# Clustered attention with a squared-ReLU MLP: another order of the opening (scales, centroids, first loads)

## The chip, the cores and the metric

The kernel runs on one core of a Trainium2 chip. The metric is the device time of one execution in microseconds. Its engines are PE (TensorE, matmuls), DVE (VectorE), ACT (ScalarE), POOL (GpSimd) and SP, which here issues all transfers.

## The reference

```python
def _attn_ref(q, k, v, centroids):            # q, k, v: 4 x 8 x 768 x 64; centroids: 8 x 16 x 64
    q_n = q / (norm(q) + 1e-06); k_n = k / (norm(k) + 1e-06); c_n = centroids / (norm(centroids) + 1e-06)
    q_assign = argmax(einsum('bhsd,hcd->bhsc', q_n, c_n), -1)
    k_assign = argmax(einsum('bhsd,hcd->bhsc', k_n, c_n), -1)
    mask = q_assign[:, :, :, None] == k_assign[:, :, None, :]
    scores = where(mask, (1 / sqrt(D)) * q @ k.T, -1e9)
    scores = scores - max(scores, -1)
    attn = exp(scores); attn = attn / (sum(attn, -1) + 1e-09)
    return attn @ v
def _moe_ref(x, w_in, w_out, s, b):           # x: 3072 x 512, w_in: 512 x 2048, w_out: 2048 x 512
    r = maximum(x @ w_in, 0.0)
    return (s * (r * r) + b) @ w_out
```

Each query attends only to the keys whose nearest centroid is the same as its own. The heads' outputs are laid side by side and go through the MLP. All inputs are float32.

## The kernel before

**The arithmetic.** Operands are scaled by a power of two and split into a high and a low float16 part, so that PE works on float16. For this, each operand needs its largest absolute value: DVE reduces along the free axis (`absmax`), PE spreads the column over all partitions (`allmax`, a matmul with the identity), DVE reduces again, and three short DVE rows (`scale2`, lines 68 to 70) make the scale of it. `split` (lines 178 to 187) then makes the high part on ACT and the low part on DVE.

**Masks.** The clusters enter the scores as extra columns: after a DMA transpose of the split keys (KA) or queries (QA), PE multiplies them by the transposed centroids cT, DVE makes a one-hot of the best cluster (`onehot`, lines 281 to 292), and this is written into a second operand, which is transposed in its turn (KB, QB). A unit's score matmuls (line 464) take QA with KA and QB with KB.

**Units and the loop.** A unit is one head, one batch and one tile of 128 queries: 192 units in all. The loop at line 709 goes over units i: score matmuls of unit i, maximum over 768 keys on DVE (line 473), exponential on ACT (line 483), transposes of the result, and the product with the values five units later. The scores have two buffers of PSUM. 21 units later the MLP of a pair of tiles begins, in steps of 128 columns of the hidden layer (lines 583, 590 to 593, 598, 610).

**Weights.** The MLP needs the largest value of all weights before its first step. The 32 weight tiles of 512 KB (w_in and w_out by turns) come through three staging buffers; for each one, ACT makes a float32 out of the loaded words (`rebase`, line 203), DVE puts the remaining bits in (`narrow`, lines 207 and 208), and ACT and PE or ACT alone bound its size (`bound`). A staging buffer is free for the next load once its tile is narrowed. Line 242, `finish_w_in`, is the first row behind the last w_in tile. The first three loads are issued in the opening, the others in the loop, two steps of the generator `weights` in each round.

**The opening.** Before the loop, lines 683 to 706 drive generators by hand: `prep_k` for the four pairs of heads of the keys (`first_k`), `prep_q` for the two halves of the first queries (`first_q`), `prep_v`, and `weights`. Each `next` takes a generator to its next `yield`: the load; absmax and allmax; scale and high part; low part and the transpose KA or QA; centroid matmuls and one-hot; the mask and the transpose KB or QB. `second` are the generators of the keys of the third and fourth pairs and of the second half of the queries.

**What sets the order.** A scheduler puts the instructions of each engine in order by priorities in the order of the program text and its own estimate of when operands are there. `behind(x, ...)` tells it to place what is inside only after the given instructions. So the order of each engine is fixed when the program is built, and an engine waits at each row until that row's operands are there, whatever stands behind it. SP issues transfers in its own fixed order too.

Of the kernel before, what the change touches and what calls it, by code (L numbers as in the profile page):

```python
# [14 lines left out]
ALU = mybir.AluOpType  # L15
# [11 lines left out]
def tile_cluster_attention_mlp(ctx, tc, q, k, v, cent, w_in, w_out, s_in, b_in, out):  # L27
    nc = tc.nc
    B, H, S, _ = q.shape
# [10 lines left out]
    V = nc.vector  # L40
# [25 lines left out]
    def scale2(dst, src):  # L66
        bits = dst.bitcast(I32)
        V.tensor_scalar(bits, src.bitcast(I32), EXPMASK, None, op0=ALU.bitwise_and)  # L68
        V.tensor_scalar(bits, bits, -1, 253 << 23, op0=ALU.mult, op1=ALU.add)
        V.tensor_scalar(dst, dst, 2.0 ** 60, None, op0=ALU.min)  # L70


    last_transpose = [None]
    last_turn = [None]
    last_split = [None, None]
    last_score = [None]
    last_max = [None]
# [45 lines left out]
    def scalar_in(src, name):  # L123
        every = const([P, 1], F32, name)
        nc.sync.dma_start(every, src.partition_broadcast(P))
        return every

    def behind(*last):
        stack = ExitStack()
        for ins in last:  # L130
            if ins is not None:
                stack.enter_context(tc.issue_after(ins.ins))
        return stack
# [7 lines left out]
    V.tensor_tensor(csq, cn, cn, op=ALU.mult)  # L141
    V.tensor_reduce(cs[:, 0:1], csq, axis=AX.X, op=ALU.add)
    A.activation(cs[:, 1:2], cs[:, 0:1], AF.Sqrt)
    for _ in range(3):
        V.tensor_scalar(cs[:, 1:2], cs[:, 1:2], 1e-30, None, op0=ALU.max)
        V.reciprocal(cs[:, 2:3], cs[:, 1:2])
        V.scalar_tensor_tensor(cs[:, 1:2], cs[:, 0:1], cs[:, 2:3], cs[:, 1:2], op0=ALU.mult, op1=ALU.add)
        V.tensor_scalar(cs[:, 1:2], cs[:, 1:2], 0.5, None, op0=ALU.mult)
# [157 lines left out]
    def prep_k(b, hp):  # L306
        kb = kb_kept
        if b == 0 and hp > 0:
            kb = sb.tile([P, 2 * T, P], F16, tag="big", name=f"kb_{hp}", bufs=BIGN).rearrange("p (h t) (e d) -> p h t e d", h=2, e=2)
        n = f"{b}_{hp}"  # L310
        kn = sb.tile([P, 2, T, D], F32, tag="kv", name=f"kn_{n}", bufs=5)
        load(kn, k[b, 2 * hp : 2 * hp + 2].rearrange("h (p t) d -> p h t d", t=T))
        yield
        if b:
            yield from until(START[b][2] if hp == 0 else step[0] + 1)
        if hp == 0:
            KSM[b] = sb.tile([P, 4, NP], F32, tag="ksm", name=f"ksm_{n}", bufs=2)
        sm = [KSM[b][:, e, hp : hp + 1] for e in range(4)]
        km = columns(1, f"k{n}")
        absmax(km, kn.rearrange("p h t d -> p (h t d)"))  # L320
        if b:
            yield
        allmax(sm[1], km, f"k{n}", "m" if b or not hp else "h")
        yield
        scale2(sm[2], sm[1])
        inverse2(V, sm[3], sm[2], 22)
        if b == 0 and hp > 0:
            ka = sb.tile([P, 2 * T, P], F16, tag="big", name=f"ka_{hp}", bufs=BIGN).rearrange("p (h t) (e d) -> p h t e d", h=2, e=2)
        else:
            ka = sb.tile([P, 2, T, 2, D], F16, tag="big", name=f"ka_{n}", bufs=BIGN)  # L330
        yield from split(ka[:, :, :, 0, :], ka[:, :, :, 1, :], kn, sm[2], False)
        G.tensor_copy(kb[:, :, :, 0, :], ka[:, :, :, 0, :])
        KA = sb.tile([P, 2 * T, P], F16, tag="KA", name=f"KA_{n}", bufs=5)
        KB = sb.tile([P, 2 * T, P], F16, tag="KB", name=f"KB_{n}", bufs=5)
        KS[(b, hp)] = (KA, KB)
        last_turn[0] = nc.sync.dma_start_transpose(KA, ka.rearrange("p h t e d -> p (h t e d)"))
        yield
        yield
        pa = (ps_m if b or not hp else ps_h).tile([P, 512], F32, tag="m" if b or not hp else "h", name=f"pk_{n}")
        for h in range(2):  # L340
            hc = slice((2 * hp + h) * C, (2 * hp + h + 1) * C)
            for t in range(T):
                i = h * T + t
                o = pa[:, i * C : (i + 1) * C]
                nc.tensor.matmul(o, KA[:, i, :], cT[:, 0, hc], start=True, stop=False)
                nc.tensor.matmul(o, KA[:, i, :], cT[:, 1, hc], start=False, stop=True)
        mk = kb.rearrange("p h t e (r c) -> p (h t) e r c", c=C)[:, :, 1, :, :]
        yield from onehot(pa, 2 * T, f"k{n}", mk, BIG, -BIG, G if b or hp > 1 else V)
        last_turn[0] = nc.sync.dma_start_transpose(KB, kb.rearrange("p h t e d -> p (h t e d)"))

    def prep_q(b, c, hq):
# [8 lines left out]
        sm = sb.tile([P, 4, 2], F32, tag="qsm", name=f"qsm_{n}", bufs=3)  # L360
# [11 lines left out]
        qa = sb.tile([P, 2 * T * P], F16, tag="big", name=f"qa_{n}", bufs=BIGN)[:, : nh * CT * 2 * D].rearrange("p (h t e d) -> p h t e d", h=nh, t=CT, e=2)  # L372
# [10 lines left out]
        QA = sb.tile([P, nh * CT, P], F16, tag="QA", name=f"QA_{n}", bufs=2)  # L383
        QB = sb.tile([P, nh * CT, P], F16, tag="QB", name=f"QB_{n}", bufs=2)
        QS[(b, c, hq)] = (QA, QB, sm)
        nc.sync.dma_start_transpose(QA, qa.rearrange("p h t e d -> p (h t e d)"))
        yield
        yield
        pa = (ps_m if b or c else ps_h).tile([P, 512], F32, tag="m" if b or c else "h", name=f"pq_{n}")
# [260 lines left out]
    wgen = weights()  # L650
# [4 lines left out]
    def run(gen):  # L655
        for _ in gen:
            pass

    def some(gen, n):
        for _ in range(n):  # L660
            next(gen, None)


    def prepare(k):
        if k == 0:
            with behind(last_transpose[0]):
                for gen in second:
                    next(gen)
        with behind(last_score[0], last_exp[0], last_max[0]):
            if k == 1:  # L670
                run(first_k[2])
                some(first_v, 1)
            if k == 2:
                run(first_k[3])
                some(first_v, 1)
            if k == 3:
                run(first_q[1])
                some(first_v, 2)
            if k == 4:
                some(first_v, 1)  # L680
                active.append(first_v)

    first_v = prep_v(0)
    first_k = [prep_k(0, hp) for hp in range(NP)]
    first_q = [prep_q(0, 0, hq) for hq in range(2)]
    second = [first_k[2], first_k[3], first_q[1]]
    for gen in (first_k[0], first_q[0], first_k[1], *second):
        next(gen)
    some(first_k[0], 2)
    some(first_k[1], 2)  # L690
    some(first_q[0], 2)
    some(first_k[0], 1)
    some(first_q[0], 1)
    some(first_k[1], 1)
    with behind(*last_split):
        for _ in range(2):
            for gen in second:
                next(gen)
    with behind(last_turn[0], *last_split):
        some(first_v, 1)  # L700
        sv = scalar_in(s_in, "sv")
        bv = scalar_in(b_in, "bv")
        some(wgen, 3)
    run(first_k[0])
    run(first_q[0])
    run(first_k[1])
    last_transpose[0] = last_turn[0]
    i = 0
    while i < NU + 8 or i - LAG < NS + 4:
# [61 lines left out]
```

## Time and profile before

| | |
|---|---|
| median of 3 runs | 953.16 us (952.39 to 954.72) |
| the profiled execution | 953.86 us, of which the profile's span is 952.2 us |
| instructions in the span | 22467 |
| first score matmul | 27.17 us |
| first maximum of scores | 34.85 us |
| first row behind the last w_in tile (line 242) | 131.37 us |
| first MLP matmul (line 583) | 133.81 us |

Times inside the span are read from its start. A busy engine may still work on what nobody waits for, so the stages have to be read one by one: the windows give each engine's busy time in a stretch, and the rows in order of time give in brackets for how long the engine had been idle and what it had waited for.

### The profile page before, as it was taken

What the parts mean: (1) busy time and instruction counts of PE and PEld (TensorE: products, weight loads), DVE (VectorE), ACT (ScalarE), POOL (GpSimd) and SP (SyncE); (2) the same over time, 40 slices, a digit from 0 to 9 for tenths busy, and PEclk for the clock granted to TensorE, in tenths of its full rate; (3) what the DMA queues carried; (4) which work ended last, traced back from release to release, by engine and by line L of the source; (5) the groups of instructions that cost most, each with busy time, mean ns of one, the idle gap of its engine ahead of it and who ended that gap; (6) DMA issues with size and microseconds to landing.
All of it is one profiled execution on the core that took longest, in us unless ns stands there. A gap on an engine that the chain in (4) does not pass through costs nothing. (4 is left out here: it accounts for less than half of the span.)

```text
span 952.2 us, 22467 instructions
## 1 busy us (share of the span) xinstructions
PE 828.6 (87%) x8625; PEld 579.4 (61%) x8625; DVE 626.1 (66%) x1400; ACT 711.0 (75%) x1390; POOL 573.0 (60%) x596
## 2 busy tenths in 40 slices
PE   0668446988999989999899999999999999999997
PEld 0457324555666667766566666766666766767764
DVE  7797988999677657767865757668666466463100
ACT  4477656887688778987787877978787888789443
POOL 3012545677578566866767758667776765676321
PEclk9965556999999999999999999999999999999999
DMA  6888974876887796968689969758877757777100
GB/s 182 227 215 234 235 179 92 197 151 114 174 167 154 170 201 122 186 147 181 139 165 177 184 142 181 149 130 189 156 153 170 145 116 152 138 165 133 33 23 22
DMA packets 450300, 147.36 MB, mean 155 GB/s; under 512 B 417937, under 2 KB 446609, under 8 KB 450193
## 3 DMA queue, kind: packets, MB, share of 16 engines
q1 hardware_dynamic: 450192, 145.93, 72.2%
q8 instruction: 67, 1.10, 0.5%
q14 instruction: 41, 0.33, 0.1%
HBM read 35.69 MB, written 6.29 MB: 44 GB/s over the span
## 5 line engine op out<-in xcount | busy, mean ns | idle before, releaser
L506 POOL TENSOR_TENSOR ph<-p,ph 128x768 f16<-128x768 f32 x184 | 312.2, 1697 | 123.7 <-ACT ph L119 76.2
L583 PE MATMUL h<-x,wis 128*128 128x256 f16 x2304 | 287.6, 274 | 9.6 <-ACT r L590 8.0
L610 PE MATMUL acc<-wos,g 128*128 128x512 f16 x1152 | 292.6, 379 | 3.2 <-POOL g L598 2.8
L583 PEld LDWEIGHTS <-wis 128*128 128x128 f16 x2304 | 222.2, 98 | 59.5 <-issue 11.3
L598 POOL TENSOR_TENSOR g<-r,g 128x256 f16<-128x256 f32 x192 | 136.6, 713 | 101.7 <-ACT r L593 97.1
L473 DVE TENSOR_REDUCE ssm<-sc 128x1 f32<-128x768 f32 x192 | 181.5, 951 | 24.4 <-PE sc L464 23.6
L483 ACT ACTIVATE p<-sc,ssm,qsm 128x768 f32<-128x768 f32 x192 | 187.7, 978 | 3.4 <-DMA PT<-ph 1.0
L610 PEld LDWEIGHTS <-g 128*128 128x128 f16 x1152 | 103.6, 97 | 87.8 <-POOL g L598 5.7
L480 ACT ACTIVATE ssm<-ssm,lift,qsm 128x1 f32<-128x1 f32 x192 | 73.1, 381 | 92.5 <-DVE ssm L473 91.7
L119 ACT ACTIVATE ph<-p 128x768 f16<-128x768 f32 x164 | 136.1, 830 | 5.8 <-DMA PT<-ph 4.3
L590 ACT ACTIVATE r<-h,cf 128x256 f32<-128x256 f32 x192 | 89.1, 464 | 56.9 <-PE h L583 49.6
L525 PE MATMUL px<-vh,PT 128*128 128x65 f16 x1104 | 120.4, 197 | 12.9 <-DVE xs L537 6.8
L464 PE MATMUL sc<-KA,QA 128*128 128x384 f16 x384 | 99.9, 343 | 26.4 <-ACT p L483 23.4
L526 PE MATMUL px<-vl,PT 128*128 128x64 f16 x1104 | 120.3, 194 | 0.0
L527 PE MATMUL px<-vh,PT 128*128 128x65 f16 x1104 | 120.0, 195 | 0.0
L525 PEld LDWEIGHTS <-PT 128*128 128x128 f16 x1104 | 103.6, 98 | 23.1 <-issue 14.4
L526 PEld LDWEIGHTS <-PT 128*128 128x128 f16 x1104 | 103.3, 100 | 13.2 <-issue 5.1
L464 PE MATMUL sc<-KB,QB 128*128 128x384 f16 x384 | 100.1, 345 | 7.0 <-DMA QB<-qb 7.0
L527 PEld LDWEIGHTS <-PT 128*128 128x128 f16 x1104 | 103.5, 98 | 2.7
L592 ACT ACTIVATE g<-r 128x256 f16<-128x256 f32 x192 | 79.3, 413 | 4.0
L593 ACT ACTIVATE r<-r 128x256 f32<-128x256 f32 x192 | 78.8, 411 | 3.3
L464 PEld LDWEIGHTS <-QA 128*128 128x128 f16 x384 | 35.9, 101 | 54.9 <-issue 29.2
(156 smaller groups left out, 1032.3 us busy)
## 6 DMA issues: line engine op xcount, KB each, us to landing
wst<-in_moe_w_in_dram SPq DMA_DIRECT2D x16, 512.0 KB, 4.5
wst<-in_moe_w_out_dram SPq DMA_DIRECT2D x16, 512.0 KB, 4.5
kn<-in_k_dram SPq DMA_DIRECT2D x16, 384.0 KB, 4.1
qn<-in_q_dram SPq DMA_DIRECT2D x24, 256.0 KB, 3.5
vn<-in_v_dram SPq DMA_DIRECT2D x16, 384.0 KB, 4.1
out_dram<-o SPq DMA_DIRECT2D x12, 512.0 KB, 3.8
PT<-ph SPq DMA_TRANSPOSE x184, 3.5
x<-xn SPq DMA_TRANSPOSE x48, 2.5
```

The source lines that it names most:

```text
L119: A.activation(dst, src, AF.Copy)
L464: last_score[0] = nc.tensor.matmul(sc[:, e, :HALF], X[:, col, :], y[:, h * S + e * HALF : h * S + (e + 1) * HALF], start=st, stop=not st)
L473: last_max[0] = V.tensor_reduce(SM[i // 4][:, 0, j : j + 1], U[i]["sc"], axis=AX.XY, op=ALU.max, negate=True)
L483: last_exp[0] = A.activation(p.rearrange("p (a b) -> p a b", a=2), u["sc"], AF.Exp, bias=bi, scale=u["scale"], **total)
L506: G.tensor_tensor(u["ph"][:, 1, :], u["p"], u["ph"][:, 0, :], op=ALU.subtract)
L525: nc.tensor.matmul(o1, PT[:, kt, :], vh[:, h, kt, : D + 1], start=(kt == 0), stop=False)
L526: nc.tensor.matmul(o, PT[:, kt, :], vl[:, h, kt, :], start=False, stop=False)
L527: nc.tensor.matmul(o1, PT[:, T + kt, :], vh[:, h, kt, : D + 1], start=False, stop=(kt == T - 1))
L583: nc.tensor.matmul(ph[:, :CW], WSP[ft][0][:, wl, kt, :], XS[(b, c, kt)][:, :, xl, :], start=(i == 0), stop=(i == len(terms) - 1))
L590: A.activation(r, ph[:, :CW], AF.Relu, scale=MS[(b, c)][0])
L598: G.tensor_tensor(g[:, 1, :], r, g[:, 0, :], op=ALU.subtract)
L610: nc.tensor.matmul(acc[:, t, :], g[:, gl, rows], WSP[ft][1][:, wl, :], start=(ft == 0 and gl + wl == 0), stop=(ft == NF - 1 and gl == 1))
```

## The change

Five things in the opening are put in another place, and one step of a root is dropped.

```diff
@@ scale2
-        V.tensor_scalar(dst, dst, 2.0 ** 60, None, op0=ALU.min)
+        return V.tensor_scalar(dst, dst, 2.0 ** 60, None, op0=ALU.min)
@@ centroids
-    for _ in range(3):
+    for _ in range(2):
         V.tensor_scalar(cs[:, 1:2], cs[:, 1:2], 1e-30, None, op0=ALU.max)
         V.reciprocal(cs[:, 2:3], cs[:, 1:2])
...
@@ prep_k
-        scale2(sm[2], sm[1])
+        last_scale[0] = scale2(sm[2], sm[1])
@@ prep_q
-        nc.sync.dma_start_transpose(QA, qa.rearrange("p h t e d -> p (h t e d)"))
+        last_q[0] = nc.sync.dma_start_transpose(QA, qa.rearrange("p h t e d -> p (h t e d)"))
@@ prepare
             if k == 1:
                 run(first_k[2])
+                some(first_q[1], 1)
                 some(first_v, 1)
             if k == 2:
                 run(first_k[3])
+                some(first_q[1], 1)
                 some(first_v, 1)
@@ the opening
-    second = [first_k[2], first_k[3], first_q[1]]
+    second = [first_k[2], first_k[3]]
     for gen in (first_k[0], first_q[0], first_k[1], *second):
         next(gen)
     some(first_k[0], 2)
-    some(first_k[1], 2)
+    with behind(last_scale[0]):
+        some(first_k[1], 2)
     some(first_q[0], 2)
     some(first_k[0], 1)
     some(first_q[0], 1)
     some(first_k[1], 1)
-    with behind(*last_split):
+    with behind(last_q[0], *last_split):
+        some(first_v, 1)
+        sv = scalar_in(s_in, "sv")
+        bv = scalar_in(b_in, "bv")
+        next(first_q[1])
+        some(wgen, 2)
         for _ in range(2):
             for gen in second:
                 next(gen)
-    with behind(last_turn[0], *last_split):
-        some(first_v, 1)
-        sv = scalar_in(s_in, "sv")
-        bv = scalar_in(b_in, "bv")
-        some(wgen, 3)
     run(first_k[0])
     run(first_q[0])
     run(first_k[1])
+    some(wgen, 1)
     last_transpose[0] = last_turn[0]
```

The maximum of the second keys is placed behind the first keys' scale. The root of the centroids' squared norms takes two Newton steps instead of three. The loads of the first values, of s and b, of the first two weight tiles and of the second half of the queries are placed behind the first transpose QA of the queries; the third weight load comes after the first one-hots. The second half of the queries is no longer prepared in the opening but in the first rounds of the loop.

In the rows below a line of the changed kernel stands two higher than the same line before, and the last number of a name is a running number. SP, the opening's transfers. kn, qn, vn are loads of keys, queries and values, wst of weights; KA, KB, QA, QB and cT are transposes. Before:

```order
L336 DMA_TRANSPOSE KA_0_1_205<-ka_1_171 128x12x128
L82 DMA vn_0_0_250<-in_v_dram 128x2x384
L125 DMA sv_252<-in_moe_s_dram 128x1
L125 DMA bv_254<-in_moe_b_dram 128x1
L82 DMA wst_0_257<-in_moe_w_in_dram 128x4x256
L160 DMA_TRANSPOSE cT_126<-cnat_120 128x3x128
L82 DMA wst_1_260<-in_moe_w_out_dram 128x1024
L82 DMA wst_2_266<-in_moe_w_in_dram 128x4x256
L386 DMA_TRANSPOSE QA_0_0_0_200<-qa_0_0_0_186 128x8x128
L349 DMA_TRANSPOSE KB_0_0_195<-kb_131 128x12x128
L399 DMA_TRANSPOSE QB_0_0_0_201<-qb_0_0_0_187 128x8x128
```

The same stretch after:

```order
L162 DMA_TRANSPOSE cT_122<-cnat_116 128x3x128
L338 DMA_TRANSPOSE KA_0_1_199<-ka_1_165 128x12x128
L351 DMA_TRANSPOSE KB_0_0_189<-kb_127 128x12x128
L388 DMA_TRANSPOSE QA_0_0_0_194<-qa_0_0_0_180 128x8x128
L84 DMA vn_0_0_203<-in_v_dram 128x2x384
L127 DMA sv_205<-in_moe_s_dram 128x1
L127 DMA bv_207<-in_moe_b_dram 128x1
L84 DMA qn_0_0_1_209<-in_q_dram 128x4x128
L84 DMA wst_0_212<-in_moe_w_in_dram 128x4x256
L84 DMA wst_1_215<-in_moe_w_out_dram 128x1024
L84 DMA wst_2_340<-in_moe_w_in_dram 128x4x256
L401 DMA_TRANSPOSE QB_0_0_0_195<-qb_0_0_0_181 128x8x128
```

QA now stands ahead of the loads of values and weights, and the first KB stands ahead of QA; the load of the second queries (qn_0_0_1), once among the first loads of the program, has come behind QA.

DVE, the rows that end in the query's mask qb, which QB transposes. pq are the query's products with the centroids, pk_0_1 those of the second keys. Before:

```order
L208 SCALAR_TENSOR_TENSOR wi1_265<-wst_2_266,wi1_265 128x512
L286 TENSOR_REDUCE om_q0_0_0_320<-pq_0_0_0_303 128x8
L287 TENSOR_TENSOR oe_q0_0_0_321<-pq_0_0_0_303,om_q0_0_0_320 128x128
L289 TENSOR_TENSOR oe_q0_0_0_321<-oe_q0_0_0_321,rev_73 128x128
L290 TENSOR_REDUCE om_q0_0_0_320<-oe_q0_0_0_321 128x8
L291 TENSOR_TENSOR oo_q0_0_0_322<-oe_q0_0_0_321,om_q0_0_0_320 128x128
L286 TENSOR_REDUCE om_k0_1_355<-pk_0_1_330 128x12
L292 TENSOR_SCALAR qb_0_0_0_187<-oo_q0_0_0_322 128x8x64
```

After:

```order
L288 TENSOR_REDUCE om_q0_0_0_291<-pq_0_0_0_274 128x8
L189 SCALAR_TENSOR_TENSOR ka_3_237<-kn_0_3_142,ksm_0_0_144,ka_3_237 128x12x64
L289 TENSOR_TENSOR oe_q0_0_0_292<-pq_0_0_0_274,om_q0_0_0_291 128x128
L291 TENSOR_TENSOR oe_q0_0_0_292<-oe_q0_0_0_292,rev_73 128x128
L292 TENSOR_REDUCE om_q0_0_0_291<-oe_q0_0_0_292 128x8
L209 TENSOR_SCALAR wi0_211<-wi0_211 128x512
L293 TENSOR_TENSOR oo_q0_0_0_293<-oe_q0_0_0_292,om_q0_0_0_291 128x128
L288 TENSOR_REDUCE om_k0_1_326<-pk_0_1_301 128x12
L210 SCALAR_TENSOR_TENSOR wi0_211<-wst_0_212,wi0_211 128x512
L294 TENSOR_SCALAR qb_0_0_0_181<-oo_q0_0_0_293 128x8x64
```

Before, all three first weight tiles are narrowed ahead of the query's one-hot; now the narrowing of the first (L209, L210) stands inside it, and that of the second and third tile behind the mask.

ACT, the rows around the exponential of the third unit, p_2. Before:

```order
L119 ACTIVATE PT_0_459<-turned_134 128x384
L483 ACTIVATE p_2_534,ssm_0_386<-sc_2_527,ssm_0_386,qsm_0_0_0_173 128x768
L203 ACTIVATE wo1_402<-wst_3_403 128x512
L480 ACTIVATE ssm_0_386<-ssm_0_386,lift_132,qsm_0_0_0_173 128x1
L483 ACTIVATE p_3_604,ssm_0_386<-sc_3_597,ssm_0_386,qsm_0_0_0_173 128x768
```

After:

```order
L205 ACTIVATE wo1_373<-wst_3_374 128x512
L205 ACTIVATE wi2_381<-wst_4_382 128x512
L217 ACTIVATE wab_3_460,l1_125<-wo1_373 128x512
L205 ACTIVATE wo2_457<-wst_5_458 128x512
L219 ACTIVATE wab_4_535<-wi2_381 128x512
L217 ACTIVATE wab_5_549,l1_125<-wo2_457 128x512
L182 ACTIVATE qn_0_0_1_209<-qn_0_0_1_209,qsm_0_0_1_419 128x256 x2
L205 ACTIVATE wi3_465<-wst_6_466 128x512
L183 ACTIVATE qb_0_0_1_510<-qn_0_0_1_209 128x4x64
L485 ACTIVATE p_2_524,ssm_0_357<-sc_2_517,ssm_0_357,qsm_0_0_0_167 128x768
```

The work on the fourth to seventh weight tiles and the scaled second half of the queries (L182, L183) has come ahead of p_2; this L182 waits for the scale that DVE makes of the second queries in the loop.

More of the change, by code (lines that the diff above doesn't have):

```diff
@@ L69, in scale2 @@
         V.tensor_scalar(bits, bits, -1, 253 << 23, op0=ALU.mult, op1=ALU.add)
-        V.tensor_scalar(dst, dst, 2.0 ** 60, None, op0=ALU.min)
+        return V.tensor_scalar(dst, dst, 2.0 ** 60, None, op0=ALU.min)
     last_transpose = [None]
     last_turn = [None]
+    last_q = [None]
+    last_scale = [None]
     last_split = [None, None]
```

## The prediction

> **What bounds the kernel now.** I read the page, then the engines by stage, then the opening in order of time, then what DVE waits for. The page:
>
> ```profile
> span 952.2 us, 22467 instructions
> PE 828.6 (87%) x8625; PEld 579.4 (61%) x8625; DVE 626.1 (66%) x1400; ACT 711.0 (75%) x1390; POOL 573.0 (60%) x596
> ```
>
> The windows (stretch, its length, busy us and instructions of each engine, granted clock, DMA share, GB/s):
>
> ```profile
> 35.00:40.00 5.00, 2.95 (x27) 1.76 (x25) 2.74 (x6) 2.82 (x6) 0.00 (x0) 1.00 1.33 231
> 40.00:85.00 45.00, 34.53 (x225) 27.77 (x223) 40.58 (x93) 33.37 (x69) 7.97 (x9) 0.69 0.81 237
> 85.00:131.40 46.40, 24.61 (x181) 17.44 (x181) 38.14 (x65) 29.05 (x58) 22.63 (x19) 0.54 1.00 242
> 160.00:875.00 715.00, 672.50 (x7368) 469.71 (x7366) 482.85 (x1057) 578.71 (x1125) 496.91 (x485) 1.00 0.78 158
> ```
>
> From 160 on PE is busy 672.5 of 715 us, 94%: whatever the opening is late or early by, the end is too. From 40 to 131.4 it is not PE but DVE that is nearly full: 40.58 + 38.14 = 78.7 of 91.4 us, 86%, with the 16 DMA engines full beside it in the second half. That stage ends when all 32 weight tiles have been loaded and narrowed. The opening in order of time (start, length; SPq rows are issues of transfers):
>
> ```profile
> 5.95 0.28 DVE L98 TENSOR_REDUCE ksm<-am_k 128x1 f32<-128x128 f32 x1
> 7.71 0.96 DVE L101 TENSOR_REDUCE amb_k<-kn 128x1 bf16<-128x768 f32 x1 [1.48 <-DMA kn<-in_k_dram]
> ...
> 9.50 1.76 ACT L185 ACTIVATE ka<-kn,ksm 128x768 f16<-128x768 f32 x2 [6.29 <-DVE ksm L70]
> ...
> 12.16 3.09 SPq L336 DMA_TRANSPOSE KA<-ka  x2
> ...
> 16.95 0.43 SPq L82 DMA_DIRECT2D wst<-in_moe_w_in_dram  x1
> ...
> 19.88 3.07 SPq L386 DMA_TRANSPOSE QA<-qa  x1
> ...
> 23.20 0.66 ACT L203 ACTIVATE wi<-wst 128x512 f32<-128x512 f32 x1 [0.29 <-DMA wst<-in_moe_w_in_dram]
> ...
> 27.17 1.46 PE L464 MATMUL sc<-KA,QA 128*128 128x384 f16 x4 [2.80 <-DMA QA<-qa]
> ...
> 28.59 1.42 SPq L349 DMA_TRANSPOSE KB<-kb  x1
> ...
> 31.22 1.23 SPq L399 DMA_TRANSPOSE QB<-qb  x1
> ...
> 33.17 1.41 SPq L349 DMA_TRANSPOSE KB<-kb  x1
> ...
> 34.85 1.82 DVE L473 TENSOR_REDUCE ssm<-sc 128x1 f32<-128x768 f32 x2 [1.70 <-PE sc L464]
> ...
> 39.19 0.53 SPq L85 DMA_DIRECT2D wst<-in_moe_w_out_dram  x1
> ...
> 131.37 0.16 DVE L242 TENSOR_REDUCE glob<-w 128x1 f32<-128x16 f32 x1
> ```
>
> To be seen here: the first query's transpose QA is issued at 19.88, behind three weight loads and the values, and PE has it at 27.17, 7.3 us later. The first maximum of scores is at 34.85, the fourth weight load at 39.19, and L242, which closes the weight stage, at 131.37. Up to L242 the built orders of before and after hold the same DVE rows but for the four rows of the dropped Newton step, so the question is only when DVE gets there.
>
> **The change part by part.** Rows for the prices (first DVE's, then what one transfer takes from issue to landing):
>
> ```profile
> 8.58 0.15 DVE L146 RECIPROCAL cs<-cs 128x1 f32<-128x1 f32 x1
> ...
> 9.32 0.14 DVE L70 TENSOR_SCALAR ksm<-ksm 128x1 f32<-128x1 f32 x1
> ...
> 12.19 1.00 DVE L187 SCALAR_TENSOR_TENSOR ka<-kn,ksm,ka 128x768 f16<-128x768 f32 x1
> ...
> 14.84 0.67 DVE L101 TENSOR_REDUCE amb_q<-qn 128x2 bf16<-128x512 f32 x1
> ...
> 17.14 0.42 DVE L98 TENSOR_REDUCE qsm<-am_q 128x2 f32<-128x256 f32 x1
> ...
> 17.60 0.33 DVE L68 TENSOR_SCALAR qsm<-qsm 128x2 int32<-128x2 int32 x1
> ...
> 23.50 0.60 DVE L64 TENSOR_SCALAR qsm<-qsm 128x2 int32<-128x2 int32 x1
> ...
> 25.47 0.42 DVE L207 TENSOR_SCALAR wi<-wi 128x512 int32<-128x512 int32 x1
> ...
> 26.40 0.68 DVE L208 SCALAR_TENSOR_TENSOR wi<-wst,wi 128x512 uint32<-128x512 uint32 x1
> 27.00 0.35 DVE L291 TENSOR_TENSOR oo_k<-oe_k,om_k 128x192 f16<-128x192 f32 x1
> ```
>
> ```profile
> wst<-in_moe_w_in_dram SPq DMA_DIRECT2D x16, 512.0 KB, 4.5
> ...
> QA<-qa SPq DMA_TRANSPOSE x24, 3.0
> ```
>
> 1. *First scale ahead of the second keys' maximum.* The scale no longer stands behind the maximum at 7.71. Its rows and those of the centroids, which took from 8.58 to 9.46, can follow the reduction at 5.95: 6.2 + 0.9 = 7.1, so ACT's first split starts 2.4 us sooner than 9.50. The second maximum is bound by its load at 7.71 and ends at 8.7; the low part (1.00) ends near 9.8 and KA goes out at 9.9 instead of 12.16.
> 2. *Two Newton steps.* Four rows of 0.15 us go, 0.6, out of a stretch in which DVE waits 1.48 for that load: worth nothing in the sum.
> 3. *Centroids and first one-hot early.* After the low part come fifteen short rows (0.15 each, 2.2), the second low part (1.0), two maxima (0.96 each) and fourteen rows of scales and one-hot (six of 0.35, eight of 0.15, 3.3): 9.8 + 8.4 = 18.2. So the first KB can go out at 18.2 instead of 28.59, and QA, now behind it on SP, at 18.2 + 1.4 = 19.6. QA is issued no sooner than 19.88; it only has no loads ahead of it and should land 3.0 later, at 22.6 instead of 27.1: 4.5 us gained there.
> 4. *Loads behind QA.* QA's own issue (1.2 as QB's) and those of values, s, b and second query (about 0.5 each, as the weight loads' 0.43 to 0.53) put the first weight load at 22.9 instead of 16.95. With 4.5 (its group) to 6.25 (16.95 to 23.20) until it is there, ACT has it between 27.4 and 29.2; I take 28.2, nearer to the group, as the transposes are done by then. ACT's 0.66 makes it 28.9. In the new DVE order its first narrowing row stands ahead of the query's mask: 0.42 + 0.68 + three rows of about 0.3 put QB at 30.9 (before 31.22). Ten more rows, four of them of the next two weight tiles, (two of 0.42, two of 0.68, six of 0.35, less the 0.06 by which neighbours overlap: 3.8) put the second KB at 34.7 (before 33.17) and the first maximum of scores right behind, 0.15 sooner than 34.85. The 4.5 us of QA are used up waiting for the weights. If this cover goes and the weights come at 29.2, all of it is 1.0 later.
> 5. *SP.* KB (1.4) and two KA (1.5 each) follow: the fourth weight load is issued at 39.1, against 39.19; that one transpose, the second query's, has left this place makes up for the later KB.
> 6. *The second query moved into the loop.* Its DVE rows leave the time before the first scores and enter the nearly full stage: 0.67 + 0.42 + six short rows of 0.15 = 2.0 us. At 86% busy I count 1.7. ACT's and POOL's part and its transposes lie beside DVE there.
>
> Sum: -0.15 + 1.7 = +1.55 us. The profiled execution took 953.86 us (its span and 1.66 around it) and would take 955.4; it lies 0.7 above the median of 953.16, on which I forecast **954.7 us**. A measurement of this kernel can tell 0.3% from no change, 2.9 us, so this is no change. The moved loads are bounded by -4.5 (all of QA's gain reaches the end) and +6.0 (all of their delay does); step 6 by 0 and +2.0.
>
> A rule speaks against part 4: the Trainium skill, "DMA: Bandwidth & Descriptors", section "Rules for kernel authors", says to issue a transfer early and wait for it late. By it the 6.0 us by which the weight loads go back would be lost and the sum be +7.5. No run here shows it so far; ACT's wait of 0.29 for the first load says that the load was not early by much before.
>
> **The rivals.** *A, faster: DVE has less to do.* The second query's six short rows from 17.60 to 23.50, which ran beside POOL's copies, took 3.65 us together (0.33 the first, 0.60 the last), against 0.9 at 0.15 each. In the loop POOL is busy 7.97 of 45 us, so 2.7 us of DVE time may vanish, and 0.6 with the Newton step. If DVE's waits stay as they are, L242 comes 3.3 us sooner: 949.9, and up to 4.5 sooner (948.7) if the weights do not hold QB. Against it: the waits don't stay, DVE idles for QA and the weights from about 20 to 28.
>
> *B, slower: the units fall behind.* In the new ACT order the third unit's exponential stands behind four weight tiles and the second query's scale.
>
> ```profile
> 41.38 0.98 ACT L483 ACTIVATE p<-sc,ssm,qsm 128x768 f32<-128x768 f32 x1
> ...
> 72.69 0.67 DVE L208 SCALAR_TENSOR_TENSOR wo<-wst,wo 128x512 uint32<-128x512 uint32 x1
> ```
>
> It (L483) ran at 41.38. Now it waits for thirty DVE rows behind the first maximum, some 16 us of work and 2 of waiting: about 53. Both score buffers are held until then. At the twelfth narrowed weight tile (before at 73.4, after by my count of the rows at 71.4) thirteen DVE rows fewer are done, the four low parts of the values (1.0 each) among them, some 7.3 us: a lag of 5.3. The forecast has DVE's later waits take most of it up:
>
> ```profile
> DVE wo L207 <- ACT wo L203: 4.0, 5, 1.2
> DVE wi L207 <- ACT wi L203: 3.7, 6, 1.6
> ```
>
> These 7.7 us are waits for weights that have just landed. If DVE finds none of them shorter, the end is 5.3 us later, 958.5. It decides from the point where DVE is busy over 95% between 60 and 131.
>
> *C, slower: PE's clock.* The granted clock fell as PE's work thinned out:
>
> ```profile
> 40.00:50.00 10.00, 9.82 (x91) 7.96 (x89) 8.24 (x17) 7.26 (x16) 1.06 (x2) 1.00 0.96 338
> 60.00:70.00 10.00, 6.69 (x34) 5.92 (x34) 9.04 (x23) 8.83 (x18) 2.28 (x3) 0.50 0.94 210
> ```
>
> With B's units gone from 40 to 53, that stretch may run at 0.50 too. Half of its 9.82 us would take 5 more; DVE's own 1.8 us of idle there hides part: +3.5, 956.7. The Trainium skill, "TensorE: Matmul & The Clock Gate", Part 1, has the clock at half after an idle window of about 3.4 us and whole after a busy one; the two rows agree with two levels.
>
> *D, slower: the late loads are paid in full,* as by the rule on early issue: +6.0 on the median, 959.2. Against it stands that nothing before QB waits for them.
>
> **How the numbers follow.** The forecast has 0.45, A 0.27, B 0.15, C 0.08, D 0.05. Faster by over 0.3% is A: 0.27. Slower by over 0.3% are B, C and D: 0.28. Same: 0.45. The range leaves out A's far end and D: 948.5 to 959.0.
>
> **What would show it.** Right: the first score matmul near 23, QB issued near 31, the first maximum near 34.7, the fourth weight load near 39, L242's counterpart near 133, and the same busy share of PE behind 160. Step 4 is wrong if QB goes out before 29 or after 32.5; step 6 if L242 comes before 130 with the first maximum where I have it. The forecast is wrong if L242 moves by over 2.9 us either way, or if the end does not follow it.

## The result, and the profile after

The changed kernel takes 966.88 us (median; 963.83 to 968.51) against 953.94 us for the kernel before, timed beside it. The ratio is 1.0127, with a 95% interval of 1.0090 to 1.0165: slower by 1.3%. The forecast of 954.7 us, and its whole range up to 959.0, were too low. The profiled execution took 967.25 us; its page begins:

```profile
span 965.4 us, 22442 instructions
PE 825.5 (86%) x8625; PEld 576.2 (60%) x8625; DVE 624.3 (65%) x1396; ACT 710.5 (74%) x1390; POOL 572.8 (59%) x596
```

No engine has more work than before, and the span is 13.2 us longer. So the time is in waits. The opening of the changed kernel, in order of time (start, length, what):

```profile
7.05 0.92 ACT L187 ACTIVATE ka<-kn,ksm 128x768 f16<-128x768 f32 x1
...
9.92 1.50 SPq L338 DMA_TRANSPOSE KA<-ka  x1
...
17.55 1.43 SPq L351 DMA_TRANSPOSE KB<-kb  x1
...
19.07 1.58 SPq L388 DMA_TRANSPOSE QA<-qa  x1
...
22.27 1.46 PE L466 MATMUL sc<-KA,QA 128*128 128x384 f16 x4 [6.48 <-DMA QA<-qa]
...
22.79 0.51 SPq L84 DMA_DIRECT2D wst<-in_moe_w_in_dram  x1
...
29.83 0.66 ACT L205 ACTIVATE wi<-wst 128x512 f32<-128x512 f32 x1 [11.21 <-DMA wst<-in_moe_w_in_dram]
...
32.29 1.23 SPq L401 DMA_TRANSPOSE QB<-qb  x1
...
35.91 0.96 DVE L475 TENSOR_REDUCE ssm<-sc 128x1 f32<-128x768 f32 x1 [0.29 <-PE sc L466]
...
55.87 0.97 ACT L485 ACTIVATE p<-sc,ssm,qsm 128x768 f32<-128x768 f32 x1
...
140.48 0.16 DVE L244 TENSOR_REDUCE glob<-w 128x1 f32<-128x16 f32 x1
```

Up to the first score matmul at 22.27 everything comes as early as the change meant it to. The first maximum of scores, at 35.91, is 1.06 us late. The row that closes the weight stage, L244, is 9.11 us late (131.37 before), and the end 13.2. The loss is therefore made in three pieces: 1.06 us by the first maximum, 8.05 us from there to L244, and 4.1 us behind it.

The second piece shows on DVE. The stretch from the first maximum to L244's counterpart, first before, then after (length; busy us of PE, PEld, DVE, ACT, POOL; granted clock; DMA share; GB/s):

```profile
34.85:131.40 96.55, 62.23 (x425) 46.98 (x424) 81.62 (x162) 65.23 (x133) 30.60 (x28) 0.64 0.93 239
```

```profile
35.90:140.50 104.60, 59.78 (x427) 43.74 (x426) 84.64 (x170) 67.09 (x138) 33.72 (x31) 0.67 0.87 222
```

DVE is busy 3.0 us longer and idle 5.0 us longer (104.60 - 84.64 = 19.96, against 96.55 - 81.62 = 14.93). What DVE waits for in that stretch (us in total, times, longest) after:

```profile
DVE ssm L475 <- PE sc L466: 5.0, 7, 1.4
DVE w L223 <- PE pw L222: 3.1, 4, 1.4
DVE PT L123 <- PE turned L505: 2.1, 2, 1.2
DVE om_k L288 <- PE pk L348: 2.0, 1, 2.0
DVE wo L209 <- ACT wo L205: 1.9, 4, 1.2
DVE wi L209 <- ACT wi L205: 1.8, 2, 1.1
```

and the longest of the waits before, other than the two for weights (4.0 and 3.7) that the prediction shows:

```profile
DVE ssm L473 <- PE sc L464: 3.4, 4, 1.7
DVE PT L121 <- PE turned L503: 1.8, 1, 1.8
DVE w L221 <- PE pw L220: 1.4, 1, 1.4
```

The waits for weights did shrink, from 7.7 to 3.7 us. But waits for PE grew in their place. The 3.4 us for scores before hold the 1.70 us that end with the first maximum itself, so they lie ahead of the stretch; after, this part is 0.29. Within the stretch the waits for scores grew from 1.7 to 4.7 us, those for the weight sums from 1.4 to 3.1, and the third pair of keys' centroid products took 2.0 in one wait.

The units fell behind first and the weights much later: the fifth maximum of scores comes at 60.12 instead of 46.45, but the 16th weight load is issued 3.2 us sooner than before and the 24th 3.7 us later. The largest single loss is at the 25th load; from there on the lag stays at 8.6 to 9.6 us up to L244. SP's rows there, before, then after:

```profile
97.50 0.52 SPq L85 DMA_DIRECT2D wst<-in_moe_w_out_dram  x1
98.24 1.24 SPq L386 DMA_TRANSPOSE QA<-qa  x1
100.56 0.37 SPq L85 DMA_DIRECT2D wst<-in_moe_w_in_dram  x1
```

```profile
101.20 0.52 SPq L87 DMA_DIRECT2D wst<-in_moe_w_out_dram  x1
109.63 0.37 SPq L87 DMA_DIRECT2D wst<-in_moe_w_in_dram  x1
110.05 1.23 SPq L388 DMA_TRANSPOSE QA<-qa  x1
```

From the 24th load to the 25th it is 3.1 us before and 8.4 after. The 25th load needs the staging buffer of the 22nd tile, which DVE frees with two rows (L207 and L208 before, L209 and L210 after). The tile's rows on ACT and DVE, with the ACT rows next to it, before:

```profile
97.32 0.65 ACT L203 ACTIVATE wo<-wst 128x512 f32<-128x512 f32 x1
97.88 0.49 ACT L544 ACTIVATE xs<-xs,vm 128x256 f32<-128x256 f32 x1
98.28 0.97 ACT L483 ACTIVATE p<-sc,ssm,qsm 128x768 f32<-128x768 f32 x1
...
98.95 0.42 DVE L207 TENSOR_SCALAR wo<-wo 128x512 int32<-128x512 int32 x1
...
99.81 0.68 DVE L208 SCALAR_TENSOR_TENSOR wo<-wst,wo 128x512 uint32<-128x512 uint32 x1
```

and after:

```profile
101.75 0.97 ACT L485 ACTIVATE p<-sc,ssm,qsm 128x768 f32<-128x768 f32 x1
...
103.02 0.49 ACT L546 ACTIVATE xs<-xs,vm 128x256 f32<-128x256 f32 x1
...
103.87 0.64 ACT L205 ACTIVATE wo<-wst 128x512 f32<-128x512 f32 x1
...
104.25 0.96 DVE L475 TENSOR_REDUCE ssm<-sc 128x1 f32<-128x768 f32 x1 [0.28 <-PE sc L466]
105.12 1.44 DVE L189 SCALAR_TENSOR_TENSOR qa<-qn,qsm,qb 128x256 f16<-128x256 f32 x2
106.48 1.86 DVE L209 TENSOR_SCALAR wo<-wo 128x512 int32<-128x512 int32 x1
108.38 1.19 DVE L210 SCALAR_TENSOR_TENSOR wo<-wst,wo 128x512 uint32<-128x512 uint32 x1
```

The tile falls behind at every step. Its load is issued 2.6 us later than before (94.31 against 91.73) and takes 6.1 us to land instead of 4.0. ACT's row of it, which stood ahead of an exponential and of L544 before, now stands behind both (L485 and L546) and is 6.6 us late. On DVE it stands behind the maximum of unit 12 (counted from 0) and the third query's low parts, and then runs in rows of 1.86 and 1.19 us that take 0.42 and 0.69 elsewhere. So it is 7.5 us late when DVE begins, and the next load is 9.1.

### The profile page after: what moved, and what is told of

Its sections match the earlier page's. It is cut to its first block, busy times and chain, and to the rows that moved or that the text cites. A ratio compares the mean times of both kernels' runs of the same rounds, so it can differ in the third digit from the quotient of the medians.

```text
span 965.4 us, 22442 instructions
## 1 busy us (share of the span) xinstructions
PE 825.5 (86%) x8625; PEld 576.2 (60%) x8625; DVE 624.3 (65%) x1396; ACT 710.5 (74%) x1390; POOL 572.8 (59%) x596
## 3 DMA queue, kind: packets, MB, share of 16 engines
HBM read 35.69 MB, written 6.29 MB: 43 GB/s over the span
## 5 line engine op out<-in xcount | busy, mean ns | idle before, releaser
L600 POOL TENSOR_TENSOR g<-r,g 128x256 f16<-128x256 f32 x192 | 134.4, 702 | 105.2 <-ACT r L595 101.4
L485 ACT ACTIVATE p<-sc,ssm,qsm 128x768 f32<-128x768 f32 x192 | 187.8, 978 | 3.6 <-PE acc L612 1.8
L466 PEld LDWEIGHTS <-QA 128*128 128x128 f16 x384 | 36.0, 102 | 55.3 <-issue 26.9
```

The lines of the kernel that those rows point to most:

```text
L466: last_score[0] = nc.tensor.matmul(sc[:, e, :HALF], X[:, col, :], y[:, h * S + e * HALF : h * S + (e + 1) * HALF], start=st, stop=not st)
L485: last_exp[0] = A.activation(p.rearrange("p (a b) -> p a b", a=2), u["sc"], AF.Exp, bias=bi, scale=u["scale"], **total)
L600: G.tensor_tensor(g[:, 1, :], r, g[:, 0, :], op=ALU.subtract)
```

## The experiments

All times are medians, each with the ratio to the kernel before timed beside it on the same chip (955 to 957 us there) and its 95% interval. "Fifth maximum" is the DVE row of the fifth unit's scores (46.45 before, 60.12 after), "stage end" is L242 before or its counterpart (131.37 and 140.48). These and all rows come from one profiled execution of each kernel, which can lie some us off its median: 5.5 us below it where the second query alone is moved, 4.3 above it with four Newton steps, 4.2 above it in the first of the runs with the third query sooner, 3.5 below it with two steps and the transpose held back.

### One part undone, one part alone

Two theories stood first. U: the second query's preparation in the loop holds the units up. W: the late loads cost. The changed kernel with the second query back in the opening:

```diff
...
             if k == 1:
                 run(first_k[2])
-                some(first_q[1], 1)
...
         for _ in range(2):
-            for gen in second:
+            for gen in [*second, first_q[1]]:
                 next(gen)
```

> The changed kernel with one part undone: the second query is prepared in the opening again (its load stays behind the first query transpose). Theory U (units held: the second query's rows in the loop stand, with four weight tiles, ahead of the units from the third on; those start 11 to 14 us late, and later weight tiles wait for them): the fifth maximum of scores comes near 48 again (before 46.45, after 60.12), the weight stage ends near 132 (before 131.37, after 140.48), and the time is 950 to 957 us. Theory W (late weight loads are what costs): still 964 to 969. Theory L (any reshuffle of the built order moves the end by a per cent): anywhere from 948 to 970, without the fifth maximum deciding it.

Measured: 967.47 us, 1.0134 (1.0112 to 1.0155); first maximum 40.83, fifth maximum 55.3, stage end 143.70. The fifth unit comes 4.8 us sooner than in the changed kernel, the first 4.9 us later, and the time stays.

The changed kernel with the loads where they were:

```diff
-    with behind(last_q[0], *last_split):
+    with behind(*last_split):
+        for _ in range(2):
+            for gen in second:
+                next(gen)
+    with behind(last_turn[0], *last_split):
         some(first_v, 1)
         sv = scalar_in(s_in, "sv")
         bv = scalar_in(b_in, "bv")
         next(first_q[1])
-        some(wgen, 2)
-        for _ in range(2):
-            for gen in second:
-                next(gen)
+        some(wgen, 3)
     run(first_k[0])
     run(first_q[0])
     run(first_k[1])
-    some(wgen, 1)
```

> The changed kernel with one part undone: the loads of values, scale, bias, second query and three weight tiles go out behind the first keys' transposes again, ahead of the first query's. Theory U: the units are held as in the changed kernel, the fifth maximum at 56 to 61, the end of the weight stage at 137 to 141, the time 961 to 968 us. Theory W: the first weight is there near 23 to 25, the weight stage ends near 132 and the time is 950 to 957.

Measured: 969.73 us, 1.0153 (1.0132 to 1.0174); first weight load at 16.4, first maximum 37.61, fifth 60.8, stage end 142.73.

The kernel before with the second query moved into the loop, and nothing else:

```diff
...
                 run(first_k[2])
+                some(first_q[1], 1)
...
-    second = [first_k[2], first_k[3], first_q[1]]
-    for gen in (first_k[0], first_q[0], first_k[1], *second):
+    second = [first_k[2], first_k[3]]
+    for gen in (first_k[0], first_q[0], first_k[1], *second, first_q[1]):
         next(gen)
```

> The kernel before with one part of the change alone: the second query is prepared in the loop (its load stays where it was). Theory U: fifth maximum at 55 to 61, weight stage ends at 137 to 141, time 961 to 968 us, so most of the change's 13 us. Theory W: 951 to 956, as before.

Measured: 969.41 us, 1.0140 (1.0118 to 1.0163); first maximum 36.50, fifth 60.05, stage end 140.22.

The kernel before with the loads behind the first query's transpose, and nothing else:

```diff
...
+        last_q[0] = nc.sync.dma_start_transpose(QA, qa.rearrange("p h t e d -> p (h t e d)"))
...
-    with behind(last_turn[0], *last_split):
+    with behind(last_q[0], *last_split):
         some(first_v, 1)
```

> The kernel before with one part of the change alone: the loads of values, scale, bias and weights wait for the first query transpose; the second query stays in the opening. Theory U: the first weight is 6 us later, but the units run as before, fifth maximum near 47, weight stage ends at 131 to 134, time 952 to 957 us. Theory W: weight stage ends near 137 to 141, time 959 to 967.

Measured: 970.42 us, 1.0158 (1.0137 to 1.0180); first maximum 42.91, stage end 144.70.

Each part alone costs as much as the whole, and undoing either gives nothing back. So prices that add up fall: the two parts alone would make 3.0%, with the whole at 1.3%. U and W fall as single causes too, with one reserve. Two of the four runs also delay the opening: the first maximum comes at 40.83 with the second query back there and at 42.91 with the loads late, 6.0 and 8.1 us behind the kernel before, so a part of what they lose is lost ahead of the loop. Against U as the only cause stand the next runs on the kernel before, whose fifth maximum is at 48 to 49 and which cost 0.8 to 1.0%.

### Edits that hardly change the work

What the four have in common is that the scheduler made another order of the whole loop. So the next runs changed the work by as little as could be. The kernel before with the first scale ahead of the second maximum:

```diff
...
+        last_scale[0] = scale2(sm[2], sm[1])
...
-    some(first_k[1], 2)
+    with behind(last_scale[0]):
+        some(first_k[1], 2)
```

> The kernel before with one part of the change alone: the first keys' scale ahead of the second keys' maximum. The four runs so far each undid or made one part and all came out 12 to 15 us above the kernel before. Theory L (the built order: the kernel before holds a placing of weight rows and units between 60 and 131 us that the scheduler gives up at almost any edit of the opening; which part is edited does not matter): 962 to 972 us, weight stage ends at 138 to 145, though the first maximum comes 1 to 2 us sooner than 34.85. Theory S (sum of parts: each moved piece has a price of its own, and this part only gains): 950 to 955, weight stage ends at 128 to 131.

Measured: 964.19 us, 1.0077 (1.0063 to 1.0091); first maximum 36.1, stage end 137.35. Its opening does not gain: the first keys' second transpose now follows three weight loads on SP, its issue takes 6.29 us, and the query's transpose stands behind it.

```profile
17.49 0.43 SPq L83 DMA_DIRECT2D wst<-in_moe_w_in_dram  x1
18.42 6.29 SPq L350 DMA_TRANSPOSE KB<-kb  x1
```

The kernel before with one Newton step less, and with one more:

```diff
-    for _ in range(3):
+    for _ in range(2):
```

> The kernel before with two Newton steps in place of three: four rows of 0.15 us less on DVE, nothing moved by hand. In its built order the centroids' rows come sooner, the first keys' second transpose leaves ahead of the first query's, and from the seventh unit on more weight tiles stand ahead of the next unit. Theory L: 960 to 972 us and the end of the weight stage at 137 to 145, though there is less work. Theory S: 952 to 956, weight stage ends at 130 to 132.

Measured: 965.71 us, 1.0099 (1.0083 to 1.0114); first maximum 37.8, stage end 136.77.

```diff
-    for _ in range(3):
+    for _ in range(4):
```

> The kernel before with four Newton steps: four rows of 0.15 us more on DVE. ACT's built order is that of the kernel before for its first 66 rows (to about 72 us) and another behind them. Theory L: 958 to 972 us, with the units level with the kernel before until 70 us and the end of the weight stage at 136 to 145. Theory S: the rows are hidden or cost 0.6 us, 953 to 956, weight stage ends at 131 to 132.

Measured: 965.24 us, 1.0096 (1.0078 to 1.0114); first maximum 37.52, fifth 49.25, stage end 137.26. Four rows of 0.15 us less cost 9 us, and four more cost 8: the work is not what costs, and what the two have in common is another order.

The changed kernel with the weights of a round placed behind that round's unit:

```diff
         background()
-        some(wgen, 2)
+        with behind(last_exp[0], last_max[0]):
+            some(wgen, 2)
```

> The changed kernel with one edit in the loop: the weight rows of a pass of the loop are placed behind the maximum and the exponential of that pass's unit, so that weights can't be put ahead of units that are due. Theory L in the form that units put behind weights are what costs: the fifth maximum comes at 50 to 56 instead of 60.1, the weight stage ends at 131 to 136 and the time is 951 to 960. Theory L in the form that only the kernel before's own placing is good: 962 to 972.

Measured: 966.67 us, 1.0104 (1.0087 to 1.0121); fifth maximum 60.4, stage end 142.10. The edit did not bring the units forward, so it says little on that form of the theory.

### The same work with the order kept

Two edits happen to keep the loop's order of the kernel before, row for row on ACT. M: the loop's order is what was lost. P: the opening pays. Two Newton steps, with the first keys' second transpose held behind the first query's:

```diff
-    for _ in range(3):
+    for _ in range(2):
...
+        last_q[0] = nc.sync.dma_start_transpose(QA, qa.rearrange("p h t e d -> p (h t e d)"))
...
-    run(first_k[0])
+    with behind(last_q[0]):
+        run(first_k[0])
```

> Two Newton steps again, and the first keys' second transpose placed behind the first query's, as it stands in the kernel before. The work is that of the run with two steps alone; but ACT's and POOL's built orders are now row for row those of the kernel before, and DVE's from the first weights on. Theory M (the order of weight rows and units in the loop is what was lost): 952 to 957 us, not measurably slower than the kernel before, weight stage ends at 130 to 133. Theory P (what counts is the opening, and an early transpose of the centroids disturbs it): the first maximum stays near 37.5 and the time at 962 to 966.

Measured: 958.58 us, 1.0032 (1.0016 to 1.0049); first maximum 37.0, stage end 133.07. Without the transpose held back the same two steps gave 1.0099. The time is above M's 952 to 957, and measurably above the kernel before; it is further below P's 962 to 966.

Five Newton steps (`range(5)`):

> Five Newton steps: eight rows of 0.15 us more on DVE than the kernel before, four more than the run with four. SP's order in the opening is that of the run with four steps (centroids' transpose behind three weight loads), but ACT's built order is row for row that of the kernel before. Theory M: the opening is 2 to 3 us late as with four steps, the first maximum near 37.5 to 38.5, the loop keeps its order, weight stage ends at 133 to 135, time 956 to 960: faster than with four steps though there is more work. Theory P: as with four steps, 964 to 968.

Measured: 957.07 us, 1.0015 (1.0005 to 1.0025); stage end 132.86. Time and stage end are as M has them. The kernel does more work than the one with four steps, its opening is as late (first maximum 37.44 against 37.52), and by the ratios it is 0.8% faster, some 8 us. Where their times part, DVE with four steps, then with five:

```profile
99.01 0.95 DVE L473 TENSOR_REDUCE ssm<-sc 128x1 f32<-128x768 f32 x1
...
102.15 0.96 DVE L473 TENSOR_REDUCE ssm<-sc 128x1 f32<-128x768 f32 x1 [1.79 <-PE sc L464]
...
103.55 2.67 DVE L187 SCALAR_TENSOR_TENSOR qa<-qn,qsm,qb 128x256 f16<-128x256 f32 x2
...
106.35 0.41 DVE L207 TENSOR_SCALAR wo<-wo 128x512 int32<-128x512 int32 x1
```

```profile
97.63 0.95 DVE L473 TENSOR_REDUCE ssm<-sc 128x1 f32<-128x768 f32 x1
...
99.49 0.87 DVE L187 SCALAR_TENSOR_TENSOR qa<-qn,qsm,qb 128x256 f16<-128x256 f32 x2
100.28 0.95 DVE L473 TENSOR_REDUCE ssm<-sc 128x1 f32<-128x768 f32 x1
101.15 0.42 DVE L207 TENSOR_SCALAR wo<-wo 128x512 int32<-128x512 int32 x1
```

With five steps the third query's low parts (L187) come ahead of the next maximum, with four behind it; there they wait 1.79 us with it for PE and then take 2.67 us instead of 0.87. The weight tile behind them (L207) starts 5.2 us later; ACT's row of it (L203) is late already, at 103.32 against 99.53. This is the place and the kind of loss that the changed kernel shows at its 25th load. It makes a part of the difference: in these two executions the stage ends 4.4 us apart, and the other 7.5 of 11.9 us arise behind it; what makes them stays open.

The scale edit with the same transpose held back (the two edits above together, three Newton steps):

> The first keys' scale ahead of the second keys' maximum, as in the change, with the first keys' second transpose placed behind the first query's; three Newton steps. ACT's built order is that of the kernel before for 74 rows, to about 80 us, DVE's last 1056 rows are the same as well. Theory M: first maximum at 32.5 to 34.5, weight stage ends at 129 to 133, time 950 to 957. Theory P: the same opening gain, time 950 to 953. Sum of parts refuted if it is above 960.

Measured: 961.88 us, 1.0063 (1.0046 to 1.0079); first maximum 36.2, stage end 135.26. Above M's number and P's: the first maximum did not gain, and the order was kept only for ACT's first 74 rows.

The kernel before with the edit of the loop that was tried on the changed one (weights behind the round's unit):

> The kernel before with an untouched opening; in the loop the weight rows of a pass are placed behind the maximum and the exponential of that pass's unit. ACT's order differs from its 14th row on, DVE's from its 55th. Theory M: first maximum within 1 us of 34.85, but the weight stage ends at 135 to 143 and the time is 959 to 968. Theory P: with the same opening 953 to 957.

Measured: 960.79 us, 1.0052 (1.0032 to 1.0072); first maximum 34.84, stage end 136.64. An untouched opening with another order of the loop is 5 us slower. That is M's side, time and stage end as it said, and P falls.

### Another loop behind the changed opening

Left open was how much of the changed kernel's own loss is its loop's order (M) and how much comes from its opening (O). The third query's preparation was started at another round; the opening stays.

```diff
-                s0 = ((b * NCH + c) * 2 + hq) * 8 - 10
+                s0 = ((b * NCH + c) * 2 + hq) * 8 - (9 if (b, c, hq) == (0, 1, 0) else 10)
```

> The changed kernel, its opening untouched; only the third query's preparation starts one pass of the loop later. ACT's order is that of the changed kernel for 72 rows, DVE's for 156, so all is the same up to about 80 us. In the changed kernel 25 weight loads lag by 1 to 5 us, and the 25th jumps to 9.1 us late, behind the maximum of unit 12 and the third query's low parts on DVE. Theory M (that jump and the 4 us behind 140 belong to the order in the loop and not to the opening): the gap from the 24th to the 25th weight load, 8.4 us in the changed kernel and 3.1 before, changes by 2 us or more, and the time leaves 964 to 969 on one side or the other. Theory O (the opening's delay is passed on and grows): gap 8 to 9, 964 to 969 us.

Measured: 964.04 us, 1.0084 (1.0054 to 1.0113); stage end 136.64. The jump is gone, as SP's rows of the 24th and 25th load show:

```profile
102.51 0.52 SPq L87 DMA_DIRECT2D wst<-in_moe_w_out_dram  x1
107.05 0.37 SPq L87 DMA_DIRECT2D wst<-in_moe_w_in_dram  x1
```

With 11 in place of 9:

> As the run before, with the third query's preparation one pass of the loop sooner; DVE's order is that of the changed kernel for 146 rows, to about 70 us. The third query's low parts and its transpose then stand ahead of the weight tiles that jumped. Theory M: gap from the 24th to the 25th load 3 to 6 us, weight stage ends at 134 to 139, time 957 to 964. Theory O: gap 8 to 9 or moved to a neighbour, weight stage ends at 140 to 142, 964 to 969 us.

Measured: 964.96 us, 1.0085 (1.0057 to 1.0113); stage end 139.57. The gap between the 24th and 25th load is 0.7 us, but the two loads before it come 6.5 and 4.2 us apart: the loss moved. PE's granted clock (third column from the end) was 1.00 from 40 to 50 and from 50 to 60, where the changed kernel's was 0.87 and 0.50, and the units were as late (fifth maximum 60.8):

```profile
50.00:60.00 10.00, 5.15 (x43) 3.76 (x43) 9.80 (x24) 6.39 (x15) 4.98 (x6) 1.00 0.81 214
```

With 12:

> As the run before, two passes sooner than in the changed kernel; DVE's order is that of the changed kernel for 123 rows, to about 62 us. Theory M: time 957 to 965 with the weight stage's end at 134 to 139; Theory O: 964 to 969.

Measured: 969.67 us, 1.0146 (1.0106 to 1.0186); stage end 140.44.

And the kernel before with 11:

> The kernel before with the third query's preparation one pass sooner, the opening untouched (first maximum at 34.85): DVE's order is that of before for 128 rows. Theory M: as its order in the loop is given up, 958 to 966 us, weight stage ends at 134 to 140. Theory O: the opening is the same, so 952 to 957.

Measured: 959.97 us, 1.0039 (1.0017 to 1.0061); first maximum 34.4, stage end 132.72.

Taken by their numbers, these runs do not settle it. Behind the changed opening the jump at the 25th load went, as M said, in one run, and moved to its neighbours, as O said, in the next. M's times did not come there: 964.04 and 964.96 lie in O's 964 to 969, and 969.67 just above it. Behind the old opening M's time came, 959.97 in 958 to 966, but not its stage end of 134 to 140: the stage ended 1.35 us later than before, and 2.5 of the 3.9 us that the profiled execution took longer arose behind it.

| opening (first maximum) | order of the loop | ratio |
|---|---|---|
| before (34.4, 34.8) | two others | 1.0039, 1.0052 |
| other Newton steps (37.0, 37.4) | that of before | 1.0032, 1.0015 |
| other Newton steps (37.5, 37.8) | two others | 1.0096, 1.0099 |
| first scale ahead (36.1, 36.2) | two others | 1.0077, 1.0063 |
| changed (35.9) | its own | 1.0127 |
| changed (35.5 to 36.4) | four others | 1.0084, 1.0085, 1.0104, 1.0146 |
| changed in part (36.5 to 42.9) | four others | 1.0134, 1.0140, 1.0153, 1.0158 |

Shown is that the loop's order moves the time with the first maximum held to within 1 us: by 4 to 5 us behind the old opening, by 6 to 8 us with other Newton steps, and by 6 us between the best and the worst of the orders behind the changed opening (964.04 and 969.67; no execution of the one reaches one of the other). No order tried behind the changed opening came below 1.0084. That opening is 1.06 us late at the first maximum and has put 2.0 us of DVE rows into the loop; this 3.1 us is about what separates the best of these from the other orders behind the old opening (1.0084 less 1.0052 is 0.3%, 3 us). That is argued and not shown. How the changed kernel's own 13 us divide between its order and its moved rows stays open: the best of the four other orders gives 3 us back, and all seven kernels that prepare the second query in the loop are at 1.0084 or above. No kernel tried beats the kernel before.

## Why the prediction was wrong

*Steps 1 and 3* were right to some tenths: ACT's first split at 7.05 (7.1), KA at 9.92 (9.9), KB at 17.55 (18.2), QA at 19.07 (19.6), landed at 22.27 (22.6).

*Step 2*, the Newton step "worth nothing in the sum", was right about its 0.6 us of work and missed what it does: alone it costs 9 us, and 3 us where the loop's order is kept.

*Step 4* had its mechanism right and one size too small. The first weight load went out at 22.79 (22.9) but ACT had it at 29.83, 7.0 us later, where 5.3 was taken and 6.25 was the far end. With the weights at 29.2, it says, "all of it is 1.0 later"; they came 0.6 us later still, and the first maximum at 35.91, 1.2 us behind the 34.7 forecast. QB at 32.29 is within the bounds that the step set itself. *Step 5* follows it: the fourth weight load is issued at 40.38 instead of 39.1.

*Step 6* is the step that failed. It priced 2.0 us of moved DVE rows at 86% and got 1.7. Where they now stand the rows took 2.75 us, and the stage lengthened by 8.05. Behind it stood the sentence that up to L242 before and after "hold the same DVE rows but for the four rows of the dropped Newton step, so the question is only when DVE gets there". The rows are the same, but not their order among each other and against PE, ACT and POOL. DVE's waits for weights were treated as a reserve of 7.7 us; 4.0 of them went, and waits for PE grew by more, so DVE's idle time rose from 14.9 to 20.0 us. That an order can cost so much is shown by the runs with four and five steps: an equal opening, four rows more in the run with five, and that one some 8 us faster. How much of the 8.05 is order and how much the moved rows stays open.

*The end follows L242*: the end moved by 13.2 and L242 by 9.1. The forecast put the stretch behind L242 at nothing. In the 40 us from 160 PE is busy 35.73 us before; in the same 40 us after the change, counted from 169.1 for the late stage, it is 33.70, so 2.0 of the 4.1 us arise there. The order differs there too; that it is the cause is not shown.

*Rival B* had the sign and the kind (units behind weights; the third unit's exponential at 55.87, about 53 expected) and 5.3 us. Its lag of the weights did not come where it had it: the twelfth tile's last narrowing row starts at 72.44, level with 72.69 before. Its own criterion did not hold: DVE is busy 59.08 of 71.4 us from 60 to 131.4, 83% and not 95%. The lag was paid because DVE idled, not because it was full. And with the fifth maximum 4.8 us sooner the time stayed, in the first run above, whose opening was late, however. *Rival A* is out: DVE's work fell by 1.8 us in the whole span (626.1 to 624.3), and the time rose. *Rival C* is out as the cause: the run with the clock at 1.00 from 40 to 60 had its fifth maximum as late (60.8) and its stage end at 139.57. *Rival D* is out as the cause of this loss: with the loads back at 16.4 the time was 969.73. Its rule (the Trainium skill, "DMA: Bandwidth & Descriptors", "Rules for kernel authors", to issue early and wait late) has a price beside its gain in the run with the first scale ahead: there the issue of a transpose right behind three early loads took 6.29 us, and 1.43 in the changed kernel, where it stands ahead of them.

*The range*, 948.5 to 959.0, is said to leave out A's far end, but 948.7 lies inside it. Nothing else hangs on this.

## What to carry to other kernels

Where a scheduler orders the instructions, an edit has two prices, its own work and the order that it sets off; here the second was ten times the first and more, and prices of parts then do not add up. To tell them apart, make an edit of next to no work, and one that does the same work but leaves the built order as it was, and time both. Idle time of an engine that feeds several others is not a reserve: before counting on it, see what stands ahead of the row that must come first, and what that row itself waits for.

## What the runs showed of the hardware

DVE rows stretch beside POOL's subtraction of the exponential's high part. In the changed kernel, L209 took 1.86 us at 106.48, when POOL ran this row:

```profile
106.36 1.69 POOL L508 TENSOR_TENSOR ph<-p,ph 128x768 f16<-128x768 f32 x1
```

The same DVE form took 0.42 us in other places. Here it ended at 108.34, 0.29 us after POOL's row (108.05), and its extra 1.44 us are about the 1.57 us that it ran beside that row. Of the 32 rows of this form up to 142 us, the 25 that took 0.41 to 0.43 us ran beside no such row of POOL, and the seven that took 0.67 to 1.86 all ran beside some row of POOL. The Trainium skill, "SBUF — State Buffer", section "Who interferes with whom", says that DVE and POOL share a pair of ports by an exclusive lock; these rows agree with it.

The loss of the changed kernel is not this stretching in sum. The kernel before has it too (1.88 us for the same form at 105.85), and from the first maximum to the end of the stage the narrowing rows took 43.2 us there and 41.9 after. Of DVE's 3.0 us of longer work in that stage 2.75 are the moved rows.
